# One-pass tanh gelu on ScalarE, residuals on VectorE, and two layers interleaved in one fixed TensorE order, in a mixer MLP kernel

## The chip, the cores and the metric

The kernel runs on one core of one Trainium2 chip. The metric is the device time of one execution in microseconds (us). Each kernel was run several times, and every experiment ran on one chip beside runs of the kernel before. The series ran on different chips, so kernels of different series are best compared by their ratios to the kernel before. "Fast" and "slow" are states of single runs: a run of this one-core program is called slow when it lies over 1.5% above the fastest run of the same kernel.

The engines are called by the profile's short names: PE is TensorE (matmul), PEld its weight loads, DVE is VectorE, ACT is ScalarE, POOL is GpSimd, SP is SyncE, which here only issues DMAs. A "hole" is a stretch in which PE is idle. PSUM is the memory in which the kernel's matmuls leave their results, and rstd is the reciprocal standard deviation that a layernorm multiplies by.

## The reference, cut to what matters

```python
B, S, D, F = 1, 2048, 512, 1792                  # bf16 throughout
h  = gelu_tanh(layernorm(x) @ w1)                # layer 1: S x D
# the four 128-column quarters of h are shifted along S by +1, -1, +2, -2 tokens, with zeros at the ends
hs = concat(shifted quarters) @ w2               # "mixing"
x1 = x + hs                                      # first residual
out = x1 + gelu_tanh(layernorm(x1) @ w3) @ w4    # layer 2: up to F, and down to D
```

The sequence is 16 tiles of 128 tokens. An "up-projection" is a matmul with w1 or w3, a "down-projection" one with w4. In matmuls of 512 columns, layer 1 has 64, mixing has 64, the layer-2 up-projection 224 and the down-projection 224: 576 in all.

## The kernel before

A small list scheduler orders each engine's work. The gelu is taken apart: ScalarE copies the accumulator out of PSUM, VectorE forms y*(y*y + k) in three passes, ScalarE takes the sigmoid, VectorE multiplies. The names c0 to c4 are the kernel's own.

```python
# c0, ScalarE:  ysb = copy(y_ps)                  1024 columns from PSUM
# c1, VectorE:  x2  = ysb * ysb
# c2a, VectorE: x2  = x2 + 1/0.044715
# c2b, VectorE: u   = x2 * ysb
sc.add("act", f"c3_{u}",
       lambda e: e.activation(sgb[:, u % NSS, 0:W], ub[:, u % NUU, 0:W],
                              ACT_F.Sigmoid, scale=GELU_C2), ...)
# c4, VectorE:  hT or h2T = ysb * sg
```

The mixing product adds its residual x on TensorE, with an identity matmul, and ScalarE evicts it:

```python
def f(e):                                          # mixing of tile t
    e.matmul(dst, ident[:], x_sb[:, t, :], start=True, stop=False)
    for j in range(DC):
        ins = e.matmul(dst, hT[:, j, c0 : c0 + P], w2_sb[:, j, :], start=False, stop=(j == DC - 1))
    ...
```

All 16 tiles of layer 1 are transposed on TensorE (64 small matmuls), all 16 of layer 2 by DMA. Layer 1 is finished first, then the 16 mixing products, then layer 2. The loads of w2, w3 and w4 are issued from POOL at points tied to that order: w3 after the last tile of layer 1 is transposed, w4 after the fifth x1.

## Time and profile before

159.37 us, median of 3 runs (159.34 to 159.63). The profiled execution spans 157.8 us.

| | before |
|---|---|
| PE, DVE, ACT busy | 138.0, 122.8, 89.7 us |
| first transpose, first up-projection | 8.41, 11.32 us |
| PE from 85 us on | dense to 154.8 us |
| last matmul to the end | 3.0 us |

From the page of the kernel before: busy time of each engine, its share of the span, and instructions; then the chain of work that ended last, by engine.

```profile
PE 138.0 (87%) x656; PEld 61.6 (39%) x656; DVE 122.8 (78%) x220; ACT 89.7 (57%) x98; POOL 19.7 (13%) x46
PE 44%; DVE 12%; issue 3%; ACT 2%; POOL 1%; POOLq 1%
```

PE is the busiest, but for 12% of the span the chain runs through DVE. Most of this are the gelu passes between 63 and 78 us.

From the groups of instructions, by shape (line, engine, operation, tiles, form and count; then busy us and mean ns of one; then idle time before it and what ended that): the two ScalarE steps of the gelu, and one of the four VectorE steps.

```profile
L449 ACT ACTIVATE ysb<-y_ps 128x1024 bf16<-128x1024 f32 x36 | 35.6, 1018 | 18.7 <-DVE h2T L497 12.1 <-PE y_ps L574 6.4
L484 ACT ACTIVATE sgb<-ub 128x2048 bf16<-128x2048 bf16 x12 | 22.9, 1910 | 9.7 <-DVE ub L477 9.7
L477 DVE TENSOR_TENSOR ub<-x2b,ysb 128x2048 bf16<-128x2048 bf16 x12 | 14.7, 1224 | 0.3
```

From the timeline of PE (start us, length us, line, operation and count): the last stretch.

```profile
121.37 33.40 PE L612 MATMUL o_ps<-w_sb,h2T 128*128 128x512 bf16 x154
```

The length includes the drain of the last matmul. The chain of waits gives this stretch 33.25 us, so 215.9 ns for each of the 154 matmuls: TensorE's pace when nothing holds it.

From the waits of PE (who waited for whom: us in total, times, longest):

```profile
PE o_ps L548 <- DVE xn_buf L425: 8.4, 1, 8.4
PE y_ps L574 <- ACT ysb L449: 3.5, 3, 1.9
PE o_ps L590 <- DVE hT L512: 2.9, 3, 1.4
```

The first line is the start; the two others are the gelu chain holding PE, by its first step (the copy comes late, since ScalarE waits for VectorE) and by its last.

### The profile page before, as it was taken

The page shows a single profiled execution, that of the slowest core. Times are in us where ns is not written, and L with a number is a line of the kernel's source. Part 1 is how long each engine was busy: PE and PEld are TensorE (multiplying, and loading weights), DVE is VectorE, ACT ScalarE, POOL GpSimd, SP SyncE. Part 2 cuts the span into 40 slices and gives each one's busy share as a digit, 9 for nine tenths or more (in the row PEclk, how much of TensorE's full clock was granted, in tenths as well). Part 3 has the DMA queues.
Part 4 walks back from the last instruction along what each step waited for, and adds up shares of the span by engine and source line. Part 5 has one row for each costly group of instructions (what it writes and reads, how often), then busy time and mean ns, then how long its engine had stood idle before and what let it go on. Part 6 is the DMA issues. An engine that isn't in the chain of part 4 may idle for free.

```text
span 157.8 us, 1825 instructions
## 1 busy us (share of the span) xinstructions
PE 138.0 (87%) x656; PEld 61.6 (39%) x656; DVE 122.8 (78%) x220; ACT 89.7 (57%) x98; POOL 19.7 (13%) x46
## 2 busy tenths in 40 slices
PE   0069989669969999995999999999999999999992
PEld 0044444224324444441443444444444444444440
DVE  0799599999999998999999999613999938922311
ACT  3074875979956555789896979610686742200000
POOL 4012542200144446000000000000000000000000
PEclk9999999999999999999999999999999999999998
DMA  5940120390069844520000000001000010110010
GB/s 145 324 196 0 41 92 2 66 396 7 2 196 301 172 73 100 101 59 0 0 2 4 0 33 0 0 33 37 34 32 0 0 66 33 37 66 33 33 66 33
DMA packets 13432, 11.12 MB, mean 70 GB/s; under 512 B 9136, under 2 KB 12208, under 8 KB 13424
## 3 DMA queue, kind: packets, MB, share of 16 engines
q1 hardware_dynamic: 12016, 6.29, 15.3%
q0 software_dynamic: 880, 4.19, 8.0%
q10 hardware_dynamic: 528, 0.52, 1.0%
q8 instruction: 5, 0.08, 0.2%
q14 instruction: 3, 0.02, 0.0%
HBM read 6.82 MB, written 2.10 MB: 56 GB/s over the span
## 4 chain that ended last, share of the span: by engine, by line
PE 44%; DVE 12%; issue 3%; ACT 2%; POOL 1%; POOLq 1%
PE o_ps L612 31%; PE y_ps L574 13%; DVE ub L477 3%; DVE x2b L462 3%; DVE h2T L497 2%; ACT ysb L449 2%; DVE x2b L469 2%; DVE xn_buf L425 1%; POOL vpe L411 1%; POOLq L728 1%; DVE st L376 1%; DVE o_sb L527 0%; DVE mv L381 0%; ACT sgb L484 0%
## 5 line engine op out<-in xcount | busy, mean ns | idle before, releaser
L574 PE MATMUL y_ps<-xnT,w_sb 128*128 128x512 bf16 x288 | 67.4, 389 | 4.6 <-ACT ysb L449 3.5
L612 PE MATMUL o_ps<-w_sb,h2T 128*128 128x512 bf16 x224 | 48.8, 379 | 0.0
L449 ACT ACTIVATE ysb<-y_ps 128x1024 bf16<-128x1024 f32 x36 | 35.6, 1018 | 18.7 <-DVE h2T L497 12.1
L484 ACT ACTIVATE sgb<-ub 128x1024 bf16<-128x1024 bf16 (+1 forms) x24 | 35.7, 1486 | 13.7 <-DVE ub L477 13.7
L574 PEld LDWEIGHTS y_ps<-xnT,w_sb 128*128 128x128 bf16 x288 | 27.5, 99 | 40.7 <-issue 5.7
L612 PEld LDWEIGHTS o_ps<-w_sb,h2T 128*128 128x128 bf16 x224 | 21.9, 98 | 26.4
L527 DVE TENSOR_TENSOR o_sb<-o_ps,x_sb 128x512 bf16<-128x512 f32 x16 | 11.0, 690 | 23.2 <-PE o_ps L612 23.1
L376 DVE BATCH_NORM_STATS2 st<-x_sb 128x6 f32<-128x512 bf16 x32 | 20.3, 671 | 5.0 <-DMA x_sb<-in_x_dram 5.0
L477 DVE TENSOR_TENSOR ub<-x2b,ysb 128x1024 bf16<-128x1024 bf16 (+1 forms) x24 | 23.0, 958 | 0.8
L462 DVE TENSOR_TENSOR x2b<-ysb 128x1024 bf16<-128x1024 bf16 (+1 forms) x24 | 22.8, 951 | 0.2
L497 DVE TENSOR_TENSOR h2T<-ysb,sgb 128x2048 bf16<-128x2048 bf16 (+1 forms) x16 | 17.2, 1084 | 0.0
L594 PE MATMUL o_ps<-w_sb,hT 128*128 128x512 bf16 x64 | 16.4, 379 | 0.0
L469 DVE TENSOR_SCALAR x2b<-x2b 128x1024 bf16<-128x1024 bf16 (+1 forms) x24 | 13.4, 560 | 0.8
L425 DVE TENSOR_SCALAR xn_buf<-x_sb,mv,rstd 128x512 bf16<-128x512 bf16 x32 | 11.7, 408 | 2.7 <-POOL rstd L416 2.4
L548 PE MATMUL o_ps<-ident,xn_buf 128*128 128x128 bf16 x56 | 5.4, 244 | 9.2 <-DVE xn_buf L425 8.4
L519 ACT ACTIVATE x_sb<-o_ps 128x512 bf16<-128x512 f32 x16 | 9.5, 596 | 5.8 <-PE o_ps L594 5.7
L416 POOL TENSOR_TENSOR rstd<-vpe,neghalf 128x2 f32<-128x2 f32 x14 | 10.6, 754 | 1.2
L558 ACT ACTIVATE xnT<-o_ps 128x512 bf16<-128x512 bf16 x14 | 7.6, 597 | 3.0 <-PE o_ps L548 2.9
L594 PEld LDWEIGHTS o_ps<-w_sb,hT 128*128 128x128 bf16 x64 | 6.3, 98 | 6.9
L548 PEld LDWEIGHTS o_ps<-ident,xn_buf 128*128 128x128 bf16 x56 | 4.1, 110 | 12.1 <-DVE xn_buf L425 8.6
L590 PE MATMUL o_ps<-x_sb,ident 128*128 128x512 bf16 x16 | 6.1, 382 | 2.9 <-DVE hT L512 2.9
L411 POOL TENSOR_SCALAR vpe<-mv 128x2 f32<-128x2 f32 x14 | 4.5, 319 | 20.2 <-DVE mv L381 20.2
(21 smaller groups left out, 24.0 us busy)
## 6 DMA issues: line engine op xcount, KB each, us to landing
w_sb<-in_w_dram POOLq DMA_DIRECT2D x2, 1792.0 KB, 8.5
out_dram<-o_sb SPq DMA_DIRECT2D x16, 128.0 KB, 1.8
x_sb<-in_x_dram SPq DMA_DIRECT2D x3, 512.0 KB, 6.8
x_sb<-in_x_dram SPq DMA_DIRECT2D x4, 128.0 KB, 4.3
w_sb<-in_w_dram ACTq DMA_DIRECT2D x1, 512.0 KB, 4.6
w_sb<-in_w_dram POOLq DMA_DIRECT2D x1, 512.0 KB, 4.2
xnT<-xn_buf SPq DMA_TRANSPOSE x16, 2.5
```

The costliest lines, as they stand in the source:

```text
L376: sc.add("dve", f"bnst{gt}", lambda e: e.bn_stats(st6[:, gt, :], src), reads=[(rsrc, 0)], writes=[(("st6", gt), 0)], dur=650)
L425: lambda e: e.tensor_scalar(xn_buf[:, gt % NXN, :], src, mv[:, gt, 0:1], rstd[:, gt : gt + 1], ALU.subtract, ALU.mult),
L449: lambda e: e.activation(ysb[:, u % NYS, GW * h : GW * (h + 1)], y_ps[:, 512 * b : 512 * b + GW], ACT_F.Copy),
L462: lambda e: e.tensor_tensor(x2b[:, u % NX2, 0:W], y, y, ALU.mult),
L469: lambda e: e.tensor_scalar(x2, x2, GELU_K, None, ALU.add),
L477: lambda e: e.tensor_tensor(ub[:, u % NUU, 0:W], x2b[:, u % NX2, 0:W], y, ALU.mult),
L484: lambda e: e.activation(sgb[:, u % NSS, 0:W], ub[:, u % NUU, 0:W], ACT_F.Sigmoid, scale=GELU_C2),
L497: sc.add("dve", f"c4_{u}", lambda e: e.tensor_tensor(dst, y, sg, ALU.mult), reads=rd, writes=w, dur=90 + 0.54 * W)
L527: lambda e: e.tensor_tensor(o_sb[:, k % NO, :], o_ps[:, 512 * (k % 2) : 512 * (k % 2 + 1)], x1_sb[:, t, :], ALU.add),
L574: ins = e.matmul(dst, wsb[:, dc, P * fc : P * (fc + 1)], srcT[:, dc, 512 * st : 512 * (st + 1)], start=(dc == 0), stop=(dc == DC - 1))
L594: ins = e.matmul(dst, hT[:, j, c0 : c0 + P], w2_sb[:, j, :], start=False, stop=(j == DC - 1))
L612: ins = e.matmul(dst, h2T[:, fc, st2 % 2, P * q : P * (q + 1)], w4_sb[:, fc, :], start=(fc == 0), stop=(fc == FC - 1))
```

## The change

It means to take VectorE off the critical path, to remove TensorE work, and to fill TensorE early by working on layer 2 while layer 1 is not finished. The whole file is rewritten; these are the parts that matter.

```diff
-    c0 Copy (ACT), c1, c2a, c2b (DVE), c3 Sigmoid (ACT), c4 (DVE)
+    pg.add("act", f"gelu{layer}_{g}_{f0}",
+           ... e.activation(d, s, ACT_F.Gelu_apprx_tanh), ...)      # straight from PSUM into hT or h2T
-    e.matmul(dst, ident[:], x_sb[:, t, :], start=True, stop=False)   # residual on PE
-    ... x1 evicted by ScalarE (Copy)
+    pg.add("dve", f"x1_{t}", ... e.tensor_tensor(x1_sb[:, t, :], dst, x_sb[:, t, :], ALU.add))
-    xnT shared by both layers, h2T for two stages of 512 tokens
+    x1nT = sb("x1nT", [P, DC, S], BF16)
+    h2T = sb("h2T", [P, FC, S], BF16)                                # the full sequence
-    64 PE transposes in layer 1
+    PE_TP = (0, 1, 2, 3, 4, 5)      # the other ten tiles by DMA transpose, issued from SP
+SCRIPT = """
+warm:9 tp:0 warm:3 tp:1 up1:0 up1:1 tp:2-3 up1:2 mix:0-1 tp:4-5 up1:3 mix:2-3 up1:4 up2:0 mix:4-5 up2:1 mix:6
+up1:5 down:0 mix:7 down:1-3 up2:2 mix:8 up1:6 mix:9-10 down:4 mix:11 down:5 mix:12 down:6 mix:13 down:7 mix:14-15
+up2:3 down:8-9 up2:4 down:10-15
+"""
...
+        load_w("pool", "w3", w3_sb, w3, 0, DC, after=[(("x", 1), 0)])
+        load_x("pool", 8, 4, after=[(("x", 7), 0)])
+        load_x("pool", 12, 4, after=[(("w3", 0), 0)])
+        load_w("pool", "w4", w4_sb, w4, 0, 7, after=[(("xT", 2, 1), 0)])
+        load_w("pool", "w4", w4_sb, w4, 7, 14, after=[(("xT", 2, 1), 0)])
```

PE runs SCRIPT in this order and no other. `up1:g` is a token group of layer 1 (groups 0 and 1 are one tile, 2 to 4 are two tiles, 5 and 6 are four), `up2:g` one of layer 2 (groups 0 and 1 are two tiles, the rest four). `warm` are matmuls of zeros. `after` says which data must have landed before the DMA is issued: w3 now goes out when tile 1 is there, and w4 when the first two tiles of layer 2 are transposed. On the other engines a scheduler sets a fixed order at build time.

## The prediction

> **What bounds it now.** The page's busy row: PE 138.0 us of 157.8, DVE 122.8, ACT 89.7. The chain of waits: from 57 to 78 us it runs through VectorE's gelu steps (x2b, ub, h2T lines, 9.9% of the span), from 85 us to the end it is TensorE alone. In the last stretch 154 matmuls take 33.25 us, 215.9 ns each: the warm gap of the Trainium skill, "TensorE: Matmul & The Clock Gate", Back-to-back issue gap (N/2.4 + 2.5 ns). So PE needs 592 x 0.216 = 127.9 us for the 512-column matmuls and some 4 us for 64 transposes. Around it: first transpose at 8.4 us, first up-projection at 11.3, about 1.7 us lost on eight matmuls at half pace (427 ns), 9 to 11 us of holes between 14 and 85 us (waits on hT, ysb, xnT), and 3.0 us after the last matmul.
>
> **What the change does.**
> 1. Gelu: Copy (36 x 1018 ns), Sigmoid (24 x 1486) and four DVE passes (about 83 us) become 36-odd ScalarE instructions from PSUM. The skill, "ScalarE: Activation LUTs", What happens when an exp ACTIVATE runs, says that throughput is one element per cycle per lane "regardless of function" (0.833 ns); the Copy fits it, so I use 1.02 us per 128x1024. ACT falls from 90 to about 43 us, DVE from 123 to about 66.
> 2. Residual: 16 identity matmuls go, -3.5 us of PE; the x1 eviction moves from ACT (596 ns) to DVE (about 690, as the final eviction).
> 3. Transposes on PE: 64 to 24, -2 us; ten layer-1 tiles go to DMA transposes (2.5 us to landing).
> 4. PE order: layer-2 work fills the layer-1 phase; 12 zero matmuls warm the clock; the first groups are one tile wide (128 columns), at most 1 us extra.
>
> DVE and ACT now have slack, so nothing but PE should bind after the start. Most of the 57 us freed on DVE buys nothing directly: only holes can go.
>
> **The sum.** PE work: 576 x 0.216 = 124.4 us. Start, by hand from the durations: x tile 0 lands near 3.5 us; each tile costs DVE about 1.3 us; first up-projection at about 7.3 us (before 11.3). Then the strict PE order waits: tiles 2 and 3 normalised near 9.7 us, the gelu before the first mixing, eviction of transposes 4 and 5 behind ScalarE's normalisations of tiles 6 and 7. I put the first layer-2 matmul at 24 to 25 us, with 10.4 us of useful matmuls before it, so about 6 us of holes. The other 114 us then run nearly dense: last matmul at 139, half-width last eviction 0.4 us, output DMA about 2.1. Span 141 to 142 us; the time before lay 1.6 us above its span: 143 us. Later holes (two PSUM banks shared by mixing and down-projection, DVE in order): 0 to 3 us; a smoother start: -3.
>
> **Predicted: 143 us, 139 to 148 (8 in 10). Chances: faster 0.98, same 0.01, slower 0.01.**
>
> **What would show it.** DVE busy 60 to 72 us, ACT 38 to 48, PE about 128 to 134. Gelu near 1.02 us per 1024. First up-projection at 7 to 8 us. PE holes of 4 to 8 us before about 25 us, under 3 us after. The chain: almost wholly PE from about 25 us on.
>
> **What would make it wrong.** The 1.8 MB w3 load starts once tile 1 has landed and could hold back x tiles 4 to 7; 26 DMA transposes in order from one queue, 1.27 us each, might land late; idle PE early could bring the half clock back; a gelu slower than the Copy; VectorE's fixed order could hold a PSUM bank.

## The result, and the profile after

154.82 us, median of 4 runs (153.69, 153.99, 155.65, 155.67), against 159.36. The ratio is 0.971 (95% interval 0.965 to 0.977). A ratio here is the mean time of one kernel's fast runs over that of the other's fast runs of the same rounds, so it is not quite the ratio of the medians. The direction was right; the gain is 4.5 us where 16 were predicted, and the time lies outside the range.

From the page of the changed kernel, the same two lines as before:

```profile
PE 137.7 (91%) x730; PEld 71.0 (47%) x730; DVE 62.1 (41%) x162; ACT 45.9 (30%) x54; POOL 20.8 (14%) x43
PE 76%; DMA 11%; DVE 5%; SPq 2%; POOL 1%; issue 1%; ACT 1%
```

DVE and ACT fell as predicted (60 to 72 and 38 to 48). The gelu costs what the Copy did (groups by shape):

```profile
L329 ACT ACTIVATE h2T<-y_ps 128x1024 bf16<-128x1024 f32 x27 | 27.6, 1024 | 64.7 <-PE y_ps L314 64.7
```

But the chain has a new member: DMA, 11%. And PE is 137.7 us busy though it has less to do; 128 to 134 were predicted. The timeline of PE shows both; in brackets is the idle time before a line and what ended it. A length includes the drain of the last matmul. The profile leaves out buffer numbers, so that x_sb stands for x1_sb too in its lines.

```profile
12.41 1.13 PE L290 MATMUL o_ps<-ident,xn_buf 128*128 128x128 bf16 x8 [3.80 <-DVE xn_buf L275]
14.23 3.60 PE L314 MATMUL y_ps<-xnT,w_sb 128*128 128x256 bf16 x16 [0.69 <-ACT xnT L295]
17.62 2.97 PE L354 MATMUL o_ps<-w_sb,hT 128*128 128x512 bf16 x8
...
22.83 1.92 PE L314 MATMUL y_ps<-xnT,w_sb 128*128 128x256 bf16 x16 [1.05 <-ACT xnT L295]
...
28.49 6.28 PE L314 MATMUL y_ps<-x1nT,w_sb 128*128 128x256 bf16 x56
34.60 1.89 PE L354 MATMUL o_ps<-w_sb,hT 128*128 128x512 bf16 x8
39.06 7.94 PE L314 MATMUL y_ps<-x1nT,w_sb 128*128 128x256 bf16 x56 [2.57 <-DMA x1nT<-xn_buf]
```

Compare equal work. The 16 matmuls at 14.23 us take 3.60 us, those at 22.83 us take 1.92. The 8 mixing matmuls take 2.97 us, then 1.89. The 56 of layer 2's first group take 6.28 us, of its second 7.94. After these two holes PE ran at half pace, though not after every hole of such a length: experiment 1 has two, of 2.99 and 2.67 us, with full pace behind them. The windows of PE's granted clock agree: 0.62 from 12 to 16 us, 0.53 from 16 to 20, 1.00 from 20 to 40, 0.57 from 40 to 44.

The chain that ended last, in order of time (start us, length us, what), says what the holes waited for:

```profile
3.64 7.49 DMA x_sb<-in_x_dram
11.13 0.02 issue
11.15 0.69 DVE st L247
11.85 0.07 DVE rstd L255
11.92 0.03 issue
11.95 0.41 DVE xn_buf L275
...
31.87 7.06 DMA x1nT<-xn_buf
38.93 0.14 issue
39.06 7.94 PE y_ps L314 x56
```

The load of x tiles 4 and 5, issued at 3.64 us, landed at 11.13. It shares the DMA engines with w3, issued at 3.61 us. DVE's order at this point is: statistics of tile 4, then the norms of tiles 2 and 3. Tiles 2 and 3 were in and their statistics done by 7.8 us, but they stood behind tile 4 in DVE's order, and PE waited for them. Later the transpose of tile 3 of layer 2 took 7.06 us, while the w4 loads, issued at 27.73 and 30.27 us, were moving; the median of these transposes is 2.5.

From here on PE has one more hole: 1.21 us at 111.5 us, for the last gelu of a group whose down-projection follows at once. The last matmul ends at 149.2 us, the prediction had 139.

### The profile page after: what moved, and what is told of

Read it like the earlier page. It is cut to its first block, busy times and chain, and to the rows that moved or that the text cites. A ratio compares the mean times of both kernels' runs of the same rounds, so it can differ in the third digit from the quotient of the medians.

```text
span 151.6 us, 1850 instructions
## 1 busy us (share of the span) xinstructions
PE 137.7 (91%) x730; PEld 71.0 (47%) x730; DVE 62.1 (41%) x162; ACT 45.9 (30%) x54; POOL 20.8 (14%) x43
## 4 chain that ended last, share of the span: by engine, by line
PE 76%; DMA 11%; DVE 5%; SPq 2%; POOL 1%; issue 1%; ACT 1%
PE y_ps L314 36%; PE o_ps L378 32%; PE o_ps L354 8%; DMA x1nT<-xn_buf 6%; DMA x_sb<-in_x_dram 5%; DVE st L247 2%; DVE xn_buf L275 2%; SPq L234 1%; POOL rstd L262 1%; ACT h2T L329 1%; POOL w_sb L239 1%; SPq L239 1%; DVE x_sb L360 0%; PE o_ps L290 0%; ACT xnT L295 0%
## 5 line engine op out<-in xcount | busy, mean ns | idle before, releaser
L314 PE MATMUL y_ps<-x1nT,w_sb 128*128 128x512 bf16 (+1 forms) x280 | 51.0, 345 | 2.6 <-DMA x1nT<-xn_buf 2.6
L378 PE MATMUL o_ps<-w_sb,h2T 128*128 128x512 bf16 (+1 forms) x238 | 49.7, 367 | 1.2 <-ACT h2T L329 1.2
L329 ACT ACTIVATE h2T<-y_ps 128x1024 bf16<-128x1024 f32 (+1 forms) x29 | 28.6, 994 | 64.7 <-PE y_ps L314 64.7
L314 PEld LDWEIGHTS y_ps<-x1nT,w_sb 128*128 128x128 bf16 x280 | 28.2, 101 | 24.9 <-issue 3.0
L386 DVE TENSOR_TENSOR o_sb<-o_ps,x_sb 128x512 bf16<-128x512 f32 (+1 forms) x17 | 11.2, 660 | 52.2 <-PE o_ps L378 52.2
L262 POOL TENSOR_TENSOR rstd<-vpe,neghalf 128x1 f32<-128x1 f32 x28 | 15.7, 563 | 66.8 <-DVE vpe L259 66.6
L360 DVE TENSOR_TENSOR x_sb<-o_ps,x_sb 128x512 bf16<-128x512 f32 x16 | 11.1, 691 | 21.8 <-PE o_ps L354 21.6
L314 PE MATMUL y_ps<-xnT,w_sb 128*128 128x256 bf16 (+2 forms) x112 | 16.6, 309 | 1.7 <-ACT xnT L295 1.7
L314 PEld LDWEIGHTS y_ps<-xnT,w_sb 128*128 128x128 bf16 x112 | 10.3, 105 | 7.4 <-ACT xnT L295 2.2
L329 ACT ACTIVATE hT<-y_ps 128x1024 bf16<-128x1024 f32 (+1 forms) x9 | 8.3, 930 | 12.5 <-PE y_ps L314 12.5
```

The costliest lines, as they stand in the source:

```text
L262: lambda e: e.tensor_tensor(rstd[:, q : q + 1], vpe[:, q : q + 1], neghalf[:], ALU.pow),
L314: ins = e.matmul(y_ps[:, p, W * i : W * (i + 1)], wsb[:, dc, P * fc : P * (fc + 1)], src[:, dc, P * t0 : P * t0 + W], start=(dc == 0), sto ...
L329: (lambda d, s: (lambda e: e.activation(d, s, ACT_F.Gelu_apprx_tanh)))(dst, ysrc),
L360: lambda e: e.tensor_tensor(x1_sb[:, t, :], dst, x_sb[:, t, :], ALU.add),
L378: ins = e.matmul(dst, h2T[:, fc, P * t : P * (t + 1)], w4_sb[:, fc, cs], start=(fc == 0), stop=(fc == FC - 1))
L386: (lambda d, c: (lambda e: e.tensor_tensor(o_sb[:, oi, c], d, x1_sb[:, t, c], ALU.add)))(dst, cs),
```

## The experiments

The theory: the change does what it should to the engines, and what is missing is lost in the first 46 us, because the loads of w3 and w4 now run against the small transfers that PE waits for, and because idle PE returns to half clock. The rivals: x and the transposes are slow by themselves; engine orders (DVE, POOL) are the limit; the streamed order is worth little and the gelu alone would have done it.

Unless said otherwise, each edit is made after the scheduler has set the order, so that the order of every engine's instructions stays as in the changed kernel, but for the moved item. All runs gave correct outputs.

### 1. w3 later, w4 later, both

```diff
         pg.order()
+        op_of = {op.name: op for op in pg.seq}
+        op_of["dma_w30"].reads.append((("x", 7), 0))               # e1: w3 waits for x tile 7, not tile 1
+        for name in ("dma_w47", "dma_w40"):                        # e2: w4 waits for tile 3 of layer 2, not tile 1
+            op = op_of[name]
+            op.reads = [(("xT", 2, 3), 0)]
+            pg.seq.remove(op)
+            pg.seq.insert(pg.seq.index(op_of["tp19"]) + 1, op)
```

> Only the start of the 1.8 MB w3 load moves, from the landing of token tile 1 to the landing of tile 7; every engine's instruction order is kept. Theory A (w3 starves the small x loads that share the DMA engines): x tile 4, which landed at 11.1 us, lands by 7 us, the 3.80 us wait of TensorE for normalised tile 2 falls below 1.5 us, the half clock at 14 to 20 us does not return (the 16 matmuls of the third group in 1.9 us, not 3.6), the first layer-2 matmul goes from 28.5 to 23-25 us, and the time from 154.8 to 149-151 us. Rival B (x is slow by itself, 1 KB rows from one queue, or the statistics chain is the limit): tile 4 still lands after 10 us, time within 1.5 us of 154.8.

> Only the start of the two w4 loads moves, from the landing of the layer-2 transpose of tile 1 to that of tile 3; every engine's instruction order is kept but for those two issues. Theory A (the w4 load slows the DMA transposes that TensorE waits for): the transpose of layer-2 tile 3 lands in 2.5 to 4 us, not 7 to 8; the wait of 2.57 us at 36.5 us is under 1 us; the half clock at 40 to 44 us does not return; time down by 3 to 4.5 us, to 150-152. Rival B (the transposes are late since they are issued in order from one queue, behind those of tiles 6 to 8): the wait at 36.5 us stays over 2 us, time within 1 us of 154.8.

> Both load moves together. If the two DMA conflicts are separate and are the whole of the missing gain, the savings add up: 154.8 - 4.5 - 3.5, so 145 to 148 us, with TensorE holes before 40 us of 4 to 6 us, as the prediction had them. If w4 now comes late for the first down-projection (needed at about 45 us), a new TensorE wait on w4 shows, and the time stays over 149.

w3 later: 150.07 us (149.79 to 151.11), ratio 0.943. w4 later: 151.79 us (151.57 to 152.13), ratio 0.953. Both: 148.60, 151.67, 151.74 and 153.24 us, one fast run, so no interval.

Timeline of PE with w3 later (same columns):

```profile
9.62 0.92 PE L290 MATMUL o_ps<-ident,xn_buf 128*128 128x128 bf16 x8 [1.37 <-DVE xn_buf L275]
11.35 2.92 PE L314 MATMUL y_ps<-xnT,w_sb 128*128 128x256 bf16 x16 [0.81 <-ACT xnT L295]
...
20.84 1.92 PE L314 MATMUL y_ps<-xnT,w_sb 128*128 128x256 bf16 x16 [2.99 <-ACT xnT L295]
...
37.18 6.27 PE L314 MATMUL y_ps<-x1nT,w_sb 128*128 128x256 bf16 x56 [2.67 <-DMA x1nT<-xn_buf]
```

The first hole fell from 3.80 to 1.37 us, and the time by 4.7 us: the w3 load was starving the x loads. DVE's statistics of tile 4 started at 8.39 us in place of 11.15 and did not wait for the load. Two things came out other than expected. The half clock still appeared, for less long (2.92 us in place of 3.60), and a new hole of 2.99 us opened before the fourth group, so layer 2 started at 26.5 us, not at 23 to 25. Behind this hole, and behind the one of 2.67 us, PE ran at full pace (1.92 and 6.27 us).

Timeline of PE with w4 later:

```profile
36.63 6.28 PE L314 MATMUL y_ps<-x1nT,w_sb 128*128 128x256 bf16 x56
42.74 1.03 PE L354 MATMUL o_ps<-w_sb,hT 128*128 128x512 bf16 x4
45.57 3.61 PE L314 MATMUL y_ps<-xnT,w_sb 128*128 128x512 bf16 x16 [1.80 <-DMA xnT<-xn_buf]
```

The hole before layer 2's second group is gone and the group runs at full pace (6.28 us), with the transposes issued from the same queue in the same order as before. So the w4 load had slowed them: the slowest layer-2 transpose up to 50 us landed after 3.0 us, where it was 8.0. It now seems to slow the next ones: PE waits 1.80 us for the layer-1 tiles 8 to 11, and the transpose that released it took 6.27 us to land (no run of its own tests this). The two savings do not add up to a stable 145 to 148 us.

### 2. The holes filled with zero matmuls, loads as in the change

```diff
+        # ("htp2", 16): before the transposes of tiles 2 and 3;  ("up2_1_0", 11): before layer 2's second group
+        def fill(e): for _ in range(n): ins = e.matmul(o_ps[:, b, :], zeros[:, 0:P], zeros[:], start=True, stop=True)
```

> The loads stay as in the changed kernel; TensorE gets 16 zero matmuls (3.5 us at full pace) in its 3.8 us hole before the transposes of tiles 2 and 3, and 11 (2.4 us) in its hole before the second layer-2 group. Theory A (an idle TensorE brings the half clock back): the holes become work that nobody needs, the 16 matmuls of the third group take 1.9 us in place of 3.6, the 8 mixing matmuls 1.9 in place of 3.0, the second layer-2 group 6.2 in place of 7.9, mean clock above 0.99, and the time falls by 3 to 4.5 us to 150.5-152, though no data come earlier. Rival B (the slow matmuls come from the DMA traffic or the operands, not from idle time): they stay slow, the time stays within 1 us.

151.09 us, median of the fast runs (150.60, 151.09, 152.31), one slow run of 153.05, ratio 0.950. The profiled execution was the slow one; from it I use only the pace of equal work in one place, not its length.

```profile
8.92 3.62 PE L449 MATMUL o_ps<-zeros 128*128 128x512 bf16 x16
12.52 0.92 PE L290 MATMUL o_ps<-ident,xn_buf 128*128 128x128 bf16 x8
14.13 1.92 PE L314 MATMUL y_ps<-xnT,w_sb 128*128 128x256 bf16 x16 [0.69 <-ACT xnT L295]
```

The 16 matmuls of the third group start at 14.13 us as in the change (14.23), with the same DMA traffic, and take 1.92 us, not 3.60. So idle time, not the data or the DMA, had brought half pace, and work that nobody needs gained over 3 us. In that execution the half clock came back once further on, from 21.7 us, so filling one hole does not end it.

### 3. One part of the change alone, on the kernel before

```diff
-                    add_c0(u, h)
-                add_c1(u); add_c2a(u); add_c2b(u); ... add_c3, add_c4
+                    add_gelu(u, h)       # e.activation(hT or h2T, y_ps, ACT_F.Gelu_apprx_tanh), up to 1024 columns
```

> The kernel before with one part of the change alone: Copy, Sigmoid and the four VectorE passes of the gelu are replaced by one tanh-gelu instruction from the PSUM accumulator per 1024 columns; identity matmuls, x1 eviction on ScalarE, 64 PE transposes, load order and layer order stay. Theory A (the gelu chain was what opened the holes of TensorE between 14 and 85 us, about 11 us): VectorE near 50 us busy, ScalarE near 55, holes before 85 us down to 2-4 us, time 148-151 us, so that this part alone gives more than the whole change did. Rival B (the layer order and the start are what the change earns by): time 154-158 us.

150.66 us (150.03 to 151.22), ratio 0.945. This one part, with the old layer order, old loads and old transposes, is 4 us better than the whole change. From its page, the busy row:

```profile
PE 136.4 (91%) x656; PEld 62.6 (42%) x656; DVE 45.4 (30%) x114; ACT 58.5 (39%) x84; POOL 17.8 (12%) x46
```

And all waits of PE that are listed for it:

```profile
PE o_ps L565 <- DVE xn_buf L425: 8.2, 1, 8.2
PE y_ps L591 <- ACT xnT L575: 0.9, 1, 0.9
```

After the first up-projection no wait of PE is listed. The holes that the gelu chain had made (3.5 and 2.9 us in the waits before, and smaller ones) are gone.

### 4. Two parts: the gelu, and the residual on VectorE

```diff
-                e.matmul(dst, ident[:], x_sb[:, t, :], start=True, stop=False)
-            sc.add("act", f"x1ev{t}", ... e.activation(x1_sb[:, t, :], o_ps[...], ACT_F.Copy)
+            sc.add("dve", f"x1ev{t}", ... e.tensor_tensor(x1_sb[:, t, :], o_ps[...], x_sb[:, t, :], ALU.add)
```

> The kernel before with two parts of the change: the one-pass gelu, and the residual added by VectorE at the eviction of the mixing product (16 identity matmuls less, 3.5 us of TensorE). Layer order, loads and transposes as before. Theory A (TensorE is the limit all along once the gelu is off VectorE): 147-148 us, 3 us less than with the gelu alone. Rival B (in the mixing phase, where the layers are not streamed, VectorE must do about 0.69 us of add plus 0.5 to 0.6 us of statistics per tile in its order, against 0.86 us of matmuls per tile, so the phase is VectorE's): the mixing phase takes 19-22 us in place of 17.3, the identity matmuls gained are given back, time 149.5-153 us.

150.40 us (149.99 to 150.75), ratio 0.947, the same as with the gelu alone, though PE has 16 matmuls less. Busy time in the mixing phase (window, its length, then PE, PEld, DVE, ACT, POOL busy us with counts, clock, DMA share, GB/s), first with the gelu alone, then with the residual too:

```profile
32.00:49.30 17.30, 17.30 (x82) 7.76 (x81) 14.15 (x38) 10.16 (x19) 6.73 (x13) 1.00 0.80 228
```

```profile
31.10:48.50 17.40, 15.69 (x64) 5.12 (x64) 16.17 (x35) 1.21 (x4) 3.93 (x7) 1.00 0.73 218
```

The phase takes 17.3 and 17.4 us. With the residual on it, DVE is busy for 16.17 of the 17.4 us, and PE has waits where it had identity matmuls. The expectation of the rival was right in kind (the gain is given back) and too high in size (19 to 22 us). In a phase that is all mixing, DVE has no time for the residual. In the streamed order mixing is spread over 80 us and it has: in the changed kernel, DVE's evictions of the mixing product wait for PE, 21.6 us in all, and PE's waits for them come to 0.6 us.

### 5. The change without streaming

```diff
-(SCRIPT as above)
+warm:9 tp:0 warm:3 tp:1 up1:0 up1:1 tp:2-3 up1:2 tp:4-5 up1:3-6 mix:0-15
+up2:0-2 down:0-3 up2:3 down:4-7 up2:4 down:8-15
```

Here the scheduler orders the other engines anew.

> The changed kernel with another PE order: all of layer 1, then the 16 mixing products, then layer 2, so no streaming of the two layers; everything else as in the change (its scheduler reorders the other engines to fit). Theory A (the streamed order asks for layer-2 transposes and for w3 and w4 while the loads run, and so is worth nothing net here): 150-155 us, no slower than the changed kernel's 154.8; in place of the holes at 20-39 us one of 4-7 us between the mixing and the first layer-2 group, for statistics, norm and transposes of the first two tiles. Rival B (streaming fills TensorE and is worth the 5 us or more that the prediction gave it): over 158 us.

164.97 us, median of the fast runs (162.85 to 165.14), ratio 1.031. My theory A fell: the streamed order is worth about 10 us to this kernel as it stands. The waits of PE in this run:

```profile
PE y_ps L313 <- DMA x1nT<-xn_buf: 6.7, 2, 4.9
PE y_ps L313 <- DMA xnT<-xn_buf: 5.4, 2, 4.3
PE o_ps L289 <- DVE xn_buf L274: 5.0, 1, 5.0
```

The hole after mixing was foreseen (4.9 us). The 5.4 us for layer 1's DMA transposes was not: without mixing and layer-2 work between, PE reaches tiles 6 to 15 before they are transposed. The mean clock was 0.937. Since experiment 3 keeps the old phase order and is fast, phases are not slow in general; they are with this kernel's ten DMA transposes and load times.

### 6. What held the fourth group, and why the fixes did not add up

> Both loads moved as in the run before, plus zero matmuls in the four holes that its trace showed (5 before the transposes of tiles 2 and 3, 2 before the third group, 9 before the fourth, 7 before the sixth; 5.0 us of work at full pace). Theory A (the spread of that kernel, 148.6 to 153.2 us, is the half clock that comes back in some executions when TensorE idles): all runs within 1 us of each other, mean clock above 0.995, median 146.5-149 us. Rival B (the spread comes from the DMA side): spread over 2 us remains.

Both loads moved, and zero matmuls in four holes (5, 2, 9 and 7 of them): 151.32 us (151.01 to 151.61), ratio 0.949. The spread did close, from 4.6 us to 0.6; but the median stayed, and the clock was 0.989. In the profiled run the fourth group starts at 21.64 us after a hole of 3.41 us, behind the nine zero matmuls, and runs at half pace:

```profile
21.64 3.48 PE L314 MATMUL y_ps<-xnT,w_sb 128*128 128x256 bf16 x16 [3.41 <-ACT xnT L295]
```

The filled holes could not bring that group forward, since an event outside PE released it: POOL's timeline has the load of tiles 12 to 15, which waits for w3 to land, and behind it in POOL's order the rstd of tile 7:

```profile
18.64 0.79 POOL L234 DMA_DIRECT2D x_sb<-in_x_dram  x1 [4.77 <-DMA w_sb<-in_w_dram]
19.45 0.57 POOL L262 TENSOR_TENSOR rstd<-vpe,neghalf 128x1 f32<-128x1 f32 x1
```

From that rstd go the norm of tile 7 on ACT, the eviction of transpose 5 behind it in ACT's order, and the fourth group. The next run takes the load of tiles 12 to 15 out of the way, with w3 late and w4 as in the change:

```diff
+        op = op_of["x_dma12"]
+        op.reads = []                                              # no wait for w3
+        pg.seq.remove(op)
+        pg.seq.insert(pg.seq.index(op_of["rstd17"]) + 1, op)       # issued after the rstd of layer-2 tile 1
```

> w3 after tile 7 as in the first run of this series, and one thing more: the load of tiles 12 to 15 does not wait for w3 in GpSimd's queue, it is issued after the layer-2 rstd of tile 1. w4 stays as in the change. Theory A (GpSimd's queue is in order, so a load waiting there held back the rstd of tile 7 and with it ScalarE's norm, transpose 5 and the fourth group): the 2.99 us hole before the fourth group falls to about 1 us, layer 2 starts at 24-25 us in place of 26.5, time 148-149 us against 150.1; the 2.7 us hole before the second layer-2 group stays, since w4 is not moved. Rival B (the hole came from VectorE's order or DMA): hole still over 2.3 us, time within 0.7 us of 150.1.

The hole fell from 2.99 to 1.05 us, and yet the kernel became slower: 151.59 and 152.74 us in its fast runs (153.92 and 154.08 in slow ones), no interval. With w3 later alone it took 149.79 to 151.11, on a chip where the kernel before took 159.42 us; on this one that took 158.87. PE's timeline of a fast run:

```profile
18.60 1.92 PE L314 MATMUL y_ps<-xnT,w_sb 128*128 128x256 bf16 x16 [1.05 <-ACT xnT L295]
...
26.00 6.28 PE L314 MATMUL y_ps<-x1nT,w_sb 128*128 128x256 bf16 x56 [1.58 <-DMA x1nT<-xn_buf]
...
38.12 7.94 PE L314 MATMUL y_ps<-x1nT,w_sb 128*128 128x256 bf16 x56 [4.12 <-DMA x1nT<-xn_buf]
```

The theory about POOL's order is shown by the fourth group. What PE gained there it lost to the next waits. A hole of 1.58 us opened before layer 2's first group: a transpose took 4.74 us to land (2.48 with w3 later), while the moved load, issued at 20.02 us, was on its way; that the load is the cause was not tested. And w4 was still in the way of the second group's transposes: the hole grew from 2.67 to 4.12 us, and after it PE ran at half pace (7.94 us for 6.27). A late wait that is longer than the time gained upstream turns the gain into idle time, and the clock adds to the bill.

### 7. All of it: a version that beats both

w3 after tile 7, the load of tiles 12 to 15 late, and w4 in seven pieces of 256 KB from ACT's queue, the first two each behind the eviction of a transpose and the others each behind one gelu, with no wait:

```diff
+        pg.seq = [op for op in pg.seq if op.name not in ("dma_w40", "dma_w47")]
+        for c, prev in enumerate(("hev4", "hev5", "gelu1_3_0", "gelu1_4_0", "gelu2_0_0", "gelu2_0_4", "gelu2_0_8")):
+            op = load_w("act", "w4_", w4_sb, w4, 2 * c, 2 * c + 2)
+            op.writes = [(("w4", i), 0) for i in (2 * c, 2 * c + 1)]
+            pg.seq.insert(pg.seq.index(op_of[prev]) + 1, op)
```

> w3 after tile 7 as before; the load of tiles 12 to 15 no longer waits for w3 in the POOL queue but is issued after the layer-2 rstd of tile 1; w4 comes in seven pieces of two rows from ScalarE's queue, spread between its gelus, with no wait. Theory A (GpSimd runs in order, so a load that waits in its queue holds back the rstd of tile 7 behind it, and from there transposes 5 and the fourth group): the hole of 2.4-3.0 us before the fourth group falls below 0.7 us, the fifth-tile eviction no longer waits, layer 2 starts at 23-24 us; with w4 in small pieces neither the transpose of layer-2 tile 3 nor those of tiles 8 to 11 hold TensorE by more than 1 us each. Time 145-148 us. Rival B (DVE's order is the limit there): the hole stays over 2 us.

Fast runs 146.07, 146.19, 146.61 us, ratio 0.918; the profiled run was slow (149.12). In it the hole before the fourth group was 1.05 us, not below 0.7 as expected, and one of 1.98 us stood before layer 2's first group, for a transpose. Then three more edits: the pieces two to three gelus later (from gelu1_4_0 to gelu2_1_4), `down:6 mix:13-15 up2:3 down:7-9 up2:4` in SCRIPT (so here the scheduler ordered the other engines anew), and zero matmuls in the first two holes.

> Aims at a version better than both. From the run with the trickled w4 (146.1 us in its fast runs): the seven w4 pieces start two to three gelus later, clear of the first layer-2 transposes, which in its profiled run held TensorE for 2.0 us; mixing of tiles 14 and 15 moves ahead of the third layer-2 group and down-projection 7 behind it, so that the down-projection which needs that group's last gelu no longer follows at once (1.2 us hole); 4 and 2 zero matmuls sit in the two first holes against the half clock. Theory A (what is left are these holes): holes at 25 us under 1 us, none near 111 us, clock above 0.995 in all runs, time 143-145.5 us. Rival B (DMA traffic holds the transposes of tiles 8 to 11 or the second layer-2 group instead): new wait on a transpose or on w4 between 33 and 48 us, time 146 us or more.

143.69 us (143.41 to 144.34), ratio 0.905. Layer 2 starts at 24.47 us. From its page, the busy row:

```profile
PE 133.1 (94%) x724; PEld 68.8 (48%) x736; DVE 61.7 (43%) x162; ACT 45.6 (32%) x54; POOL 19.1 (13%) x41
```

And the longest waits of PE, but for the 1.2 us ahead of the first zero matmuls:

```profile
PE y_ps L314 <- ACT xnT L295: 1.1, 1, 1.1
PE o_ps L290 <- DVE xn_buf L275: 1.0, 3, 0.6
PE y_ps L314 <- DMA x1nT<-xn_buf: 0.9, 1, 0.9
```

Are the six zero matmuls needed? The same kernel without them:

> The 143.7 us version without its six added zero matmuls (1.3 us of work in two holes near 8 and 11 us); nothing else differs. Theory A (they keep the clock up): in some or all executions the half clock returns between 11 and 20 us, the mean clock is below 0.99 there and the time is 1 to 3 us longer, 144.5-147 us, with more spread. Rival B (the loads and the order did it all): 143-144 us in all runs, clock as before.

144.58 us median (143.61 to 145.14), ratio 0.906 with an interval of 0.902 to 0.910, against 0.905 (0.903 to 0.908): no difference that these runs can show. With x in time the first hole was 0.52 us in the profiled run and the third group took 1.92 us anyway. The loads and the order did it.

## Why the prediction was wrong

Its sum had three parts: a start up to the first layer-2 matmul at 24 to 25 us, 114 us run "nearly dense" from there, and a tail of 2.5 us. Each is set against the traces.

- **The work on the engines: right.** DVE 62.1, ACT 45.9 us; the gelu 1.02 us per 1024 columns. The Trainium skill, "ScalarE: Activation LUTs", Step-by-step: what each stage is for, says the rate does not depend on the function (the prediction names the heading before it); the gelu at 1024 ns and the Copy at 1018 agree. PE's full pace was right too, 216 ns per 512 columns, and 32 matmuls of 128 columns took under 2 us.
- **First up-projection at 7.3 us: right**, 6.66 us.
- **The first step that failed: "I put the first layer-2 matmul at 24 to 25 us".** It was 28.49. The holes on the way add up to what I had put down, 3.80 + 0.69 + 0.56 + 1.05 + 0.25 = 6.35 us against 6. But the sum priced every matmul at full pace. Third group and first mixing ran at half pace after the first hole: 6.2 us from 14.23 to 20.43 for 16 x 0.108 + 8 x 0.216 = 3.5 us of work, so 2.7 us lost. The rest is drains at each hole, and transposes at half pace. That the sum of the holes matches is luck: I had tiles 2 and 3 normalised near 9.7 us, and it was 12.9. I followed them through DVE with durations alone; the order put tile 4's statistics ahead of them, and tile 4 came late.
- **The second step: "The other 114 us then run nearly dense".** It took 120.7 us (28.49 to 149.17). 2.57 us are the wait for the transpose of tile 3, 1.7 us the half clock after it (7.78 us to the next matmul for 56 x 0.108 = 6.0), 1.2 us the gelu wait at 111.5 us. Some 1.2 us are not accounted for. The later holes that I had allowed for, PE waiting for a PSUM bank, do not show among the waits of its matmuls after the start; its weight loads for the down-projection waited 1.7 us in all for DVE's evictions.
- **The run.** The profiled run was the fastest of four, 153.69 us; the median is 1.1 us higher. The time lay 2.1 us above the span, where I had 1.6.
- **The hazards were named and not priced.** "What would make it wrong" lists w3 holding back x tiles 4 to 7, late DMA transposes, and the half clock. All three happened, and the sum held no term for any of them. The signs were to be had: in the trace before, these transposes took 2.5 us in the median and 6.0 at most, and the first eight up-projection matmuls ran at 427 ns.

The Trainium skill, "DMA: Bandwidth & Descriptors", Issuing engines are not separate DMA queues, says that DMAs from all issuing engines run on the same 16 engines and interleave. Here moving one 1.8 MB load by some 6 us, with nothing else moved, cut the first hole from 3.80 to 1.37 us. "TensorE: Matmul & The Clock Gate", Architectural detail, says that ACT and DVE take instructions strictly in order; the norms of tiles 2 and 3, at 11.95 and 12.47 us behind tile 4's statistics at 11.15, agree.

With these conflicts removed the design runs at 143.7 us, and layer 2 starts at 24.47 us. This is near the prediction, but it took four edits to get there, so it shows that the term for the work was sound, not that the forecast of this kernel was. Left open: the 1.2 us above; why single executions of the changed kernel fall near 153.7 to 154.0 or near 155.7 us (their mean clocks, 0.965 to 0.978, do not order them); how the gain from 146.2 to 143.7 us divides between the later w4 pieces and the moved mixing, as these ran together; what DVE's order alone costs at the first hole, since no run moved the two norms ahead of tile 4; what decides after which holes PE falls to half pace; and what the streamed order is worth once the loads are out of the way.

## What to carry to other kernels

When a change lets TensorE start later work earlier, it moves that work's loads earlier too: list every transfer that is in flight when TensorE waits for a small one, and give the bulk load a later start or small pieces. On an engine with a fixed order look at what stands in front of the instruction that matters, above all one that waits for a DMA. And test the parts alone: one part of this change, the gelu, was worth more than the whole, and another, the residual, was worth nothing without the new order; within it, it was not run alone.

## What the Trainium skill lacked or had wrong

- "TensorE: Matmul & The Clock Gate", Back-to-back issue gap, gives 131 ns per matmul as the sustained pace at 512 columns. Here it was 215.9 ns over 154 matmuls, which is what the section gives for the isolated gap, about 216 ns. For 128 columns it gives 81 ns with weight loads; 32 of them, each with its weight load, took 1.95 us here, at most 61 ns each.
- The same page, HAM oscillation, puts the return to the half clock at idle gaps over about 3.4 us. The change fits at its first hole (3.80 us, then 3.60 us in place of 1.92), but not at its second (2.57 us, then 7.94 us in place of 6.28). With w3 later, holes of 1.37 and 0.81 us with eight transposes between them were followed by a third group of 2.92 us, and longer ones of 2.99 and 2.67 us by full pace. So the length of the last gap did not decide it here. (Another section of the page allows for short idles that come often, so the page as a whole does not exclude this.) No run here shows what decides.
- "DMA: Bandwidth & Descriptors", Rules for kernel authors, says that a transpose next to ordinary DMAs needs nothing. That is about correct results, which these runs had. Beyond the shared engines, no page says by how much bulk loads slow it. Transposes of one 128 KB tile landed after 2.5 us in the median and after 8.0 us at most beside the w4 load.
- The skill has the strict order of an engine's instructions, but no page draws the conclusion that a DMA which waits in POOL's order holds back POOL's arithmetic behind it. Here waits of 4.77 us, and of 3.59 us with w3 later alone, did, and moving that load cut a hole on TensorE from 2.99 to 1.05 us.
